# Decoding float64 weight chunks in pairs, in pieces of 512 columns, in place in a ring of four staged chunks

## The chip, the cores and the metric

The kernel runs on one core of one Trainium2 chip, in one launch. The metric is the device time of the whole program in microseconds (us). It is written by hand in a tile framework that keeps one instruction queue per engine: TensorE (PE, with its weight loads PEld), VectorE (DVE), ScalarE (ACT), GpSimd (POOL) and SyncE (SP, which issues most DMAs). Each engine runs its queue in order; an instruction that waits holds up everything behind it on its engine. The framework fixes the order in every queue when the program is built.

## The reference, cut to what matters

Three stages follow each other. The first is a recurrent attention over 4 batches, 8 heads, 768 tokens and 48 dimensions. The second is a feed-forward network on 3072 tokens, whose two weights are the subject here. The third is a mixture of 8 experts.

```
h = x @ w_in                       # w_in 384 x 2048
g = where(h > 0, h, exp(min(h, 0)) - 1)
x = g @ w_out                      # w_out 2048 x 384
```

The two weights arrive as float64 (they are drawn in float32 and multiplied by a float64 scalar). The kernel reads each float64 as two 32-bit words, the high and the low one, and forms from them the bits of a float32.

## The kernel before, in words

**Tiles.** The attention works on 24 tiles of 128 tokens (6 chunks of time, 4 batches) in four steps A1 to A4. Its result, transposed, is xT. The feed-forward network takes two tiles at a time: 12 groups of 256 tokens, each in 8 units. `ffn_in` (L537, 18 matmuls per unit into a PSUM bank psf) multiplies by one eighth of w_in, three instructions on ACT and DVE (L544, L545, L546) apply the nonlinearity, ACT and POOL split the result into a high and a low fp16 part (L548, L335), and two units later `ffn_out` (L561, 12 matmuls into the accumulators pso) multiplies by one eighth of w_out. There are three accumulators and a group uses two, so the next group needs one of them free: after the last unit of a group, L569 on ACT and L570 on DVE read them out. A mixture-of-experts stage follows with its own weights.

**The weights of the feed-forward network** stay in SBUF as fp16 pairs, wi and wo, 8 chunks of 768 columns each. These 16 chunks are made while the first group runs, in the order wi0, wi1, wi2, wo0, wi3, wo1, and so on to wo7; SEQ holds that list, and below chunk k is its k-th entry from 0. For each chunk:
- SP loads 768 KB (1536 32-bit words on each of 128 partitions) into a buffer stg (L261). There are three buffers. The load of chunk k waits until DVE has read chunk k-3 out of the buffer.
- DVE decodes it in two pieces of 384 columns with three instructions each. L283 and L284 read the high words, which lie 8 bytes apart, and leave bits in pt, a part of a PSUM accumulator bank that the first group does not use. L285 reads the low words, combines them with pt and writes float32 into a separate packed tile, sti, of which there are two buffers.
- ACT scales sti in place (L297) and copies it to the high fp16 part (L300). POOL subtracts to get the low fp16 part (L301).

**What sets the order.** A list of due times in the program (start, steps) places the attention steps among the units. The framework's own model of durations then settles the order in each engine's queue. Around the decode, DVE also runs the attention's scans (L349), masks (L449), products (L354, L355), outputs (L500, L505) and the setup of the router (L227 to L249). `early.close()` (L1070) gives back the memory of stg and sti after the first group.

## Time and profile before

| | us |
|---|---|
| median of 3 runs | 756.91 |
| lowest and highest of them | 754.46, 759.87 |
| profiled execution, its own time | 758.86 |
| its span, first to last instruction | 757.0 |

The span is divided by engine: PE is busy 94% of it, DVE 69%, ACT 65%, POOL 53%. Busy shares are averages over stages with different limits, so the stretches of the span have to be read apart. The decode of the 16 chunks lies between 12.6 and 98.8 us of the span.

### The profile page before, as it was taken

How to read it: one execution, taken by the hardware profiler on the slowest of the kernel's cores; microseconds unless marked ns; L12 is line 12 of the kernel's file. 1: busy time of each engine (PE TensorE's matmuls, PEld its weight loads, DVE VectorE, ACT ScalarE, POOL GpSimd, SP SyncE). 2: the span in 40 equal slices, each digit the busy share in tenths (PEclk: the TensorE clock that was granted, in tenths of full speed). 3: DMA queues.
4: the chain of work that ended last, by engine and by line, in shares of the span. 5: the costliest groups of instructions: out<-in, count | busy, mean ns of one | idle time of the engine just before them, and what ended most of it. 6: DMA issues, size and time to landing. Idle time of an engine off the chain costs nothing.

```text
span 757.0 us, 17652 instructions
## 1 busy us (share of the span) xinstructions
PE 710.9 (94%) x6769; PEld 536.6 (71%) x6769; DVE 521.6 (69%) x1080; ACT 490.2 (65%) x951; POOL 405.0 (53%) x414
## 2 busy tenths in 40 slices
PE   4899998999999999999999999998897999999984
PEld 4768766777777777776777777775675777777763
DVE  5999794666756675668566745776787688767751
ACT  3578646577666666666666766466744789767752
POOL 5878689778687767777767660021025433331211
PEclk9999899999999999999999999999998999999998
DMA  9975343353323432344231102199439999999820
GB/s 283 278 231 178 115 113 80 109 107 116 92 80 88 132 70 81 100 122 100 80 78 54 33 13 33 53 260 289 141 107 233 346 300 378 300 270 271 254 82 13
DMA packets 89059, 114.77 MB, mean 152 GB/s; under 512 B 60709, under 2 KB 67018, under 8 KB 88964
## 3 DMA queue, kind: packets, MB, share of 16 engines
q1 hardware_dynamic: 84512, 102.75, 48.6%
q0 software_dynamic: 3456, 10.24, 4.5%
q8 instruction: 57, 0.93, 0.5%
q10 hardware_dynamic: 996, 0.53, 0.3%
q14 instruction: 38, 0.31, 0.1%
HBM read 90.29 MB, written 9.84 MB: 132 GB/s over the span
## 4 chain that ended last, share of the span: by engine, by line
PE 55%; DMA 17%; DVE 13%; issue 6%; ACT 5%; POOL 2%; SPq 1%; POOLq 0%; DVEq 0%; ACTq 0%
PE psf L537 19%; PE pso L561 19%; DMA out_dram<-ob,idxb 7%; PE pso L894 4%; DMA SG<-in_w_dram 3%; DMA wi<-in_w_dram 3%; PE psf L874 3%; PE psa L443 2%; DVE RK L349 1%; DVE W L866 1%; ACT W L865 1%; PE psa L440 1%; DMA wi<-scr,idxa 1%; PE psa L874 1%; PE psa L519 1%
## 5 line engine op out<-in xcount | busy, mean ns | idle before, releaser
L537 PE MATMUL psf<-xT,wi 128*128 128x256 f16 x1728 | 212.6, 277 | 5.5 <-DVE e L546 3.6
L561 PE MATMUL pso<-wo,ring 128*128 128x384 f16 x1152 | 212.0, 327 | 5.9 <-DVE X L570 3.3
L537 PEld LDWEIGHTS <-wi 128*128 128x128 f16 x1728 | 167.3, 99 | 34.3 <-issue 4.5
L561 PEld LDWEIGHTS <-ring 128*128 128x128 f16 x1152 | 109.7, 98 | 69.5 <-issue 5.7
L335 POOL TENSOR_TENSOR ring<-e,ring 128x512 f16<-128x512 f32 x80 | 92.9, 1164 | 61.2 <-ACT ring L548 58.5
L546 DVE SCALAR_TENSOR_TENSOR e<-e,psf 128x512 f32<-128x512 f32 x96 | 65.7, 684 | 85.1 <-ACT e L545 79.0
L894 PE MATMUL pso<-W,gg 128*128 128x384 f16 x624 | 112.3, 328 | 1.7 <-DVE gg L335 1.6
L874 PEld LDWEIGHTS <-W 128*128 128x128 f16 x1008 | 93.4, 99 | 24.1 <-DMA XM<-G 5.0
L548 ACT ACTIVATE ring<-e 128x512 f16<-128x512 f32 x96 | 60.2, 627 | 61.1 <-DVE e L546 61.0
L894 PEld LDWEIGHTS <-gg 128*128 128x128 f16 x624 | 60.6, 98 | 37.6 <-DVE gg L335 2.9
L902 POOL DMA_INDIRECT out_dram<-ob,idxb x20 | 25.2, 1261 | 95.8 <-DVE ob L901 33.5
L544 ACT ACTIVATE e<-psf 128x512 f32<-128x512 f32 x96 | 56.5, 589 | 27.2 <-PE psf L537 23.0
L545 ACT ACTIVATE e<-e,nel 128x512 f32<-128x512 f32 x96 | 69.0, 719 | 2.5
L866 DVE SCALAR_TENSOR_TENSOR W<-wi,W 128x768 f16<-128x768 f32 x56 | 52.0, 953 | 21.7 <-ACT W L865 20.4
L866 DVE SCALAR_TENSOR_TENSOR W<-SG,W 128x768 f16<-128x768 f32 x56 | 52.5, 953 | 16.0 <-ACT W L865 15.9
L874 PE MATMUL psf<-XM,W 128*128 128x256 f16 (+1 forms) x540 | 60.5, 262 | 0.5 <-ACT mt L880 0.2
L335 DVE TENSOR_TENSOR gg<-mt,gg 128x256 f16<-128x256 f32 (+1 forms) x112 | 43.5, 402 | 22.6 <-ACT gg L881 22.0
L865 ACT ACTIVATE W<-wi 128x768 f16<-128x768 f32 x56 | 45.3, 837 | 17.7 <-DMA wi<-in_w_dram 13.4
L865 ACT ACTIVATE W<-SG 128x768 f16<-128x768 f32 x56 | 45.9, 836 | 16.3 <-DMA SG<-in_w_dram 15.1
L880 ACT ACTIVATE mt<-psf 128x256 f32<-128x256 f32 (+1 forms) x84 | 29.6, 360 | 30.8 <-PE psf L874 23.2
L881 ACT ACTIVATE gg<-mt 128x256 f16<-128x256 f32 (+1 forms) x112 | 42.6, 397 | 1.6
L349 DVE TENSOR_TENSOR_SCAN RK<-lw,bnd 112x520 f32<-112x520 f32 x24 | 34.3, 1430 | 7.0 <-ACT lw L348 4.8
(266 smaller groups left out, 1147.8 us busy)
## 6 DMA issues: line engine op xcount, KB each, us to landing
SG<-in_w_dram SPq DMA_DIRECT2D x28, 768.0 KB, 7.3
wi<-in_w_dram SPq DMA_DIRECT2D x28, 768.0 KB, 6.6
stg<-in_w_in_dram SPq DMA_DIRECT2D x8, 768.0 KB, 5.9
stg<-in_w_out_dram SPq DMA_DIRECT2D x8, 768.0 KB, 4.4
ld<-in_rk_dram SPq DMA_DIRECT2D x16, 384.0 KB, 3.2
lw<-in_w_dram SPq DMA_DIRECT2D x24, 227.5 KB, 3.2
lr<-in_r_dram SPq DMA_DIRECT2D x24, 224.0 KB, 3.6
lk<-in_k_dram SPq DMA_DIRECT2D x24, 224.0 KB, 3.1
```

The lines of the kernel that those rows point to most:

```text
L335: (nc.gpsimd if pool else nc.vector).tensor_tensor(lo, f, hi, op=ALU.subtract)
L537: mm = nc.tensor.matmul(ph[:, 256 * z_:256 * z_ + 256], lhsT=wi[:, u_, a, kk, 128 * z_:128 * z_ + 128], rhs=xg[:, b_ * KD + kk, :], start= ...
L544: nc.scalar.activation(e, ph, AF.Exp, scale=_pow2(-PH))
L545: nc.scalar.activation(e, e, AF.Identity, scale=_pow2(PH), bias=nel)
L546: LASTV[0] = nc.vector.scalar_tensor_tensor(e, e, 0.0, ph, op0=ALU.min, op1=ALU.max).ins
L548: LASTA[0] = nc.scalar.activation(hl[:, 0], e, AF.Copy).ins
L561: nc.tensor.matmul(po_[g][i][:, 0:DM], lhsT=hl[:, a, z_, 128 * i:128 * i + 128], rhs=wo[:, u_, b_, z_, :], start=(u_ + z_ + n == 0), stop= ...
L865: nc.scalar.activation(o_[:, 0], i_, AF.Copy, scale=_pow2(sc))
L866: nc.vector.scalar_tensor_tensor(o_[:, 1], i_, _pow2(sc), o_[:, 0], op0=ALU.mult, op1=ALU.subtract)
L874: nc.tensor.matmul(ph[:, 0:n_], lhsT=w_[:, a, kk, 128 * m:128 * m + 128], rhs=xm[:, b_ * KD + kk, 0:n_], start=(n == 0), stop=(n == 3 * KD ...
L881: nc.scalar.activation(h2[:, 0, m, 0:n_], t_, AF.Copy)
L894: MK[0] = nc.tensor.matmul(po[:, 0:DM], lhsT=h2[:, a, m, 128 * t:128 * t + 128], rhs=w_[:, b_, m, :], start=(m == 0 and a + b_ == 0), stop ...
```

## The change

The three buffers stg and the two buffers sti, together 24,576 bytes on each partition, become one tile stg of the same size: a ring of four chunks. Chunk k lies in slot k mod 4. Chunks 0 and 1 are decoded as before, each in two pieces of 384 columns. From chunk 2 on, an even chunk and the odd one after it lie in neighbouring slots and are decoded as one run of 1536 columns in three pieces of 512: two pieces when the even chunk's turn comes, the third when the odd one's does. The second piece covers the last 256 columns of the even chunk and the first 256 of the odd one, so both must have been loaded. pt is now a whole PSUM bank of 512 columns.

The last instruction of a piece writes the float32 over the low words, 8 bytes apart. ACT scales them there in place, ACT and POOL read them there. So a slot comes free only when POOL has subtracted its chunk. Four chunks are loaded at the start, where it was three; afterwards the loads of a pair are written in the program just before the pair's first piece.

In the changed file the three decode instructions are L275, L276 and L277, the load is L268, and the scaling, copy and subtraction are L309, L312 and L313. Every line behind them has a number higher by 12.

```diff
--- before.py
+++ after.py
@@ -254,40 +254,52 @@
     PDT = ["o2"]
     LASTD = [None]
 
+    NSG, CW = 4, 768
+    stg = s0.tile([128, NSG * CW * (2 if wide else 1)], I32 if wide else F32, name="stg", bufs=1)
+    DV = {}
+
+    def slot(k):
+        w_ = CW * (2 if wide else 1)
+        return stg[:, w_ * (k % NSG):w_ * (k % NSG) + w_]
+
     def prep_load(key):
         i = key[1]
-        src = (wiv if key[0] == 0 else wov)[i]
-        st = s0.tile([128, 768 * z], I32 if wide else F32, tag="stg", name="stg", bufs=3)
-        nc.sync.dma_start(st, src)
+        st = slot(SEQ.index(key))
+        nc.sync.dma_start(st, (wiv if key[0] == 0 else wov)[i])
         staged[key] = st
+
+    def decode(o, n):
+        sv = stg.rearrange("p (x t) -> p x t", t=2)
+        h_, l_ = sv[:, o:o + n, 1], sv[:, o:o + n, 0]
+        pt = OB[2].bitcast(I32)[:, 0:n]
+        nc.vector.tensor_scalar(pt, h_, 3, 0x3FFFFFFF, op0=ALU.logical_shift_left, op1=ALU.bitwise_and)
+        nc.vector.scalar_tensor_tensor(pt, h_, -0x40000000, pt, op0=ALU.bitwise_and, op1=ALU.bitwise_or)
+        LASTD[0] = nc.vector.scalar_tensor_tensor(
+            l_, l_, 29, pt, op0=ALU.logical_shift_right, op1=ALU.bitwise_or
+        ).ins
 
     def prep(n, dst, key, sc, mode):
         mode = int(mode)
-        if key not in staged:
-            prep_load(key)
-        st = staged[key]
         k0 = SEQ.index(key)
-        prep_(n, dst, st, sc, mode)
-        for q in range(k0 + 1, min(k0 + 1 + PLD, len(SEQ))):
+        for q in range(k0, min(k0 + (1 if k0 < 2 or k0 % 2 else 2), len(SEQ))):
             if SEQ[q] not in staged:
                 prep_load(SEQ[q])
-
-    def prep_(n, dst, st, sc, mode):
+        o = CW * (k0 % NSG)
         if wide:
-            t = s0.tile([128, 768], I32, tag="sti", name="sti")
-            sv = st.rearrange("p (x t) -> p x t", t=2)
-            hi, lo = sv[:, :, 1], sv[:, :, 0]
-            for o in (0, 384):
-                pt = psum(PDT[0]).bitcast(I32)[:, 0:384]
-                h_, l_ = hi[:, o:o + 384], lo[:, o:o + 384]
-                nc.vector.tensor_scalar(pt, h_, 3, 0x3FFFFFFF, op0=ALU.logical_shift_left, op1=ALU.bitwise_and)
-                nc.vector.scalar_tensor_tensor(pt, h_, -0x40000000, pt, op0=ALU.bitwise_and, op1=ALU.bitwise_or)
-                LASTD[0] = nc.vector.scalar_tensor_tensor(
-                    t[:, o:o + 384], l_, 29, pt, op0=ALU.logical_shift_right, op1=ALU.bitwise_or
-                ).ins
-            t = t.bitcast(F32)
+            if k0 < 2:
+                decode(o, 384)
+                decode(o + 384, 384)
+            elif k0 % 2 == 0:
+                decode(o, 512)
+                decode(o + 512, 512)
+            else:
+                decode(o + 256, 512)
+            t = stg.bitcast(F32).rearrange("p (x t) -> p x t", t=2)[:, o:o + CW, 0]
         else:
-            t = st
+            t = slot(k0)
+        prep_(n, dst, t, sc, mode)
+
+    def prep_(n, dst, t, sc, mode):
         fv = t.rearrange("p (a c) -> p a c", a=n)
         if mode == 0:
             nc.scalar.activation(dst[:, 0], fv, AF.Copy, scale=_pow2(sc))
@@ -1033,7 +1045,7 @@
             SEQ.append((0, u_))
         if u_ >= LAG:
             SEQ.append((1, u_ - LAG))
-    for key in SEQ[:3]:
+    for key in SEQ[:4]:
         prep_load(key)
     pq = [0]
 
```

DVE's queue, around the product L355 (L367 now) that ends the first use of a psf bank by the attention; RK, lw and psf are attention tiles, pso_69 is pt. Before:

```order
L283 TENSOR_SCALAR pso_69<-stg 128x384
L284 SCALAR_TENSOR_TENSOR pso_69<-stg,pso_69 128x384
L354 SCALAR_TENSOR_TENSOR RK_103<-RK_103,psf 112x8x64
L285 SCALAR_TENSOR_TENSOR sti<-stg,pso_69 128x384
L355 SCALAR_TENSOR_TENSOR RK_103<-RK_103,psf 112x8x64
```

and now:

```order
L275 TENSOR_SCALAR pso_69<-stg 128x512
L276 SCALAR_TENSOR_TENSOR pso_69<-stg,pso_69 128x512
L277 SCALAR_TENSOR_TENSOR stg<-stg,pso_69 128x512
L275 TENSOR_SCALAR pso_69<-stg 128x512
L276 SCALAR_TENSOR_TENSOR pso_69<-stg,pso_69 128x512
L277 SCALAR_TENSOR_TENSOR stg<-stg,pso_69 128x512
L366 SCALAR_TENSOR_TENSOR RK_103<-RK_103,psf 112x8x64
L275 TENSOR_SCALAR pso_69<-stg 128x512
L367 SCALAR_TENSOR_TENSOR RK_103<-RK_103,psf 112x8x64
```

In the whole queue ahead of this product stood 36 decode instructions of 384 columns (chunks 0 to 5); now 12 of 384 and 22 of 512 stand there (chunks 0 to 5, and four instructions of the pair 6 and 7).

SP's queue, around the loads of chunks 4 to 8, with what each waits for; lv, lk and lr are loads of the attention. Before:

```order
L261 DMA stg<-in_w_in_dram 128x1536 [waits DMAHW3_49,DVE_49]
L331 DMA lv<-in_v_dram 128x384 [waits DMAHW4_49,PE_49,Pool_49]
L261 DMA stg<-in_w_out_dram 128x1536 [waits DMAHW5_49,DVE_49]
L331 DMA lv<-in_v_dram 128x384 [waits DMAHW6_49,PE_49,Pool_49]
L261 DMA stg<-in_w_in_dram 128x1536 [waits DMAHW7_49,DMAHW0_49,DVE_49]
L331 DMA lk<-in_k_dram 112x512 [waits Pool_49]
L331 DMA lr<-in_r_dram 112x512 [waits DMAHW1_49,Pool_49]
```

and now:

```order
L268 DMA stg<-in_w_out_dram 128x1536 [waits DMAHW5_49,Pool_49]
L343 DMA lv<-in_v_dram 128x384 [waits DMAHW6_49,PE_49]
L268 DMA stg<-in_w_in_dram 128x1536 [waits DMAHW7_49,Pool_49]
L343 DMA lk<-in_k_dram 112x512 [waits DMAHW0_49,Pool_49]
L343 DMA lr<-in_r_dram 112x512 [waits DMAHW1_49,Pool_49]
L268 DMA stg<-in_w_out_dram 128x1536 [waits DMAHW2_49,DVE_49,Pool_49]
L268 DMA stg<-in_w_in_dram 128x1536 [waits DMAHW3_49,Pool_49]
```

The loads of the weights waited for DVE, and now wait for POOL; the attention's loads lk and lr still stand behind one of them.

ACT's queue, ahead of the first reading out of an accumulator, L569 (L581 now); X_107 is what it writes, ubc, Tk and Tr belong to the attention. Before:

```order
L471 ACTIVATE Ss_112<-US_110 112x192
L548 ACTIVATE ring<-e 128x512
L402 ACTIVATE Tk<-lk 112x512
L1074 ACTIVATE ubc<-ubc 128x384
L402 ACTIVATE Tr<-lr 112x512
L569 ACTIVATE X_107<-pso_67 128x384
```

and now:

```order
L375 ACTIVATE pso_68<-RK_103 112x4
L556 ACTIVATE e<-psf 128x512
L557 ACTIVATE e<-e,nel 128x512
L581 ACTIVATE X_107<-pso_67 128x384
L483 ACTIVATE Ss_112<-US_110 112x192
L560 ACTIVATE ring<-e 128x512
```

Tk and Tr stood ahead of the reading out, and now stand behind it; ubc is done earlier.

## Rows read from the trace of the kernel before

**Rows 1.** The page: busy us, share of the span, instructions of each engine.
```profile
PE 710.9 (94%) x6769; PEld 536.6 (71%) x6769; DVE 521.6 (69%) x1080; ACT 490.2 (65%) x951; POOL 405.0 (53%) x414
```

**Rows 2.** Busy time of each engine by stretch (x instructions), granted clock, DMA.
```profile
core 0: us, PE busy (x) PEld busy (x) DVE busy (x) ACT busy (x) POOL busy (x), PEclk, DMA share, GB/s
20.00:25.00 5.00, 5.00 (x34) 4.73 (x34) 4.93 (x6) 0.77 (x3) 5.00 (x4) 1.00 1.10 281
15.00:100.00 85.00, 78.80 (x580) 64.01 (x578) 77.39 (x138) 55.81 (x100) 64.98 (x60) 0.96 0.62 194
75.00:80.00 5.00, 4.28 (x40) 3.60 (x40) 4.93 (x10) 4.28 (x10) 4.84 (x5) 0.78 0.68 217
80.00:85.00 5.00, 5.00 (x25) 3.27 (x24) 2.87 (x6) 2.29 (x4) 2.99 (x4) 0.54 0.43 150
94.00:115.20 21.20, 18.18 (x146) 13.28 (x145) 18.84 (x29) 11.46 (x24) 16.95 (x17) 1.00 0.39 101
120.00:140.00 20.00, 19.61 (x198) 15.55 (x198) 10.28 (x18) 10.81 (x20) 15.32 (x17) 1.00 0.28 71
```

**Rows 3.** The chain of waits up to 140 us: start us, us, what.
```profile
43.11 0.69 DVE RK L355
...
43.84 3.71 PE psf L537 x18
...
80.07 3.84 PE psf L537 x18
...
113.23 0.41 ACT ubc L1074
113.65 0.52 ACT Tr L402
...
114.57 0.57 DVE X L570
...
115.19 1.14 PE pso L561 x6
```

**Rows 4.** Groups of DVE by form, to 110 us: count, busy us, mean ns, idle.
```profile
L283 DVE TENSOR_SCALAR pso<-stg 128x384 int32<-128x384 int32 x32 | 17.9, 558 | 1.7 <-DMA stg<-in_w_in_dram 1.0
L284 DVE SCALAR_TENSOR_TENSOR pso<-stg,pso 128x384 int32<-128x384 int32 x32 | 17.8, 558 | 0.7
L285 DVE SCALAR_TENSOR_TENSOR sti<-stg,pso 128x384 int32<-128x384 int32 x32 | 17.5, 548 | 1.0
...
L449 DVE SCALAR_TENSOR_TENSOR Ab<-psa,cs 128x512 f32<-128x512 f32 x8 | 5.5, 685 | 1.2 <-PE psa L440 1.2
```

**Rows 5.** Order of time (start us, us, what): first matmuls of the first group.
```profile
38.92 4.00 PE L537 MATMUL psf<-xT,wi 128*128 128x256 f16 x18 [0.90 <-ACT xT L377]
```

**Rows 6.** What DVE waited for, 12 to 116 us: us, times, longest.
```profile
DVE e L546 <- ACT e L545: 2.9, 2, 2.5
DVE X L570 <- ACT X L569: 1.9, 1, 1.9
```

**Rows 7.** Order of time, from one chunk's last decode to its subtraction.
```profile
63.73 0.55 DVE L285 SCALAR_TENSOR_TENSOR sti<-stg,pso 128x384 int32<-128x384 int32 x1
...
65.49 0.83 ACT L297 ACTIVATE sti<-sti 128x768 f32<-128x768 f32 x1
...
66.35 0.84 ACT L300 ACTIVATE wo<-sti 128x768 f16<-128x768 f32 x1
...
67.27 1.65 POOL L301 TENSOR_TENSOR wo<-sti,wo 128x768 f16<-128x768 f32 x1 [0.20 <-ACT pso L363]
```

**Rows 8.** The tile stg: time from issue to landing.
```profile
DMA to landing us min/median/max: 4.2/4.6/9.8
```

**Rows 9.** Groups of ACT at other strides and sizes, to 100 us.
```profile
L297 ACT ACTIVATE sti<-sti 128x768 f32<-128x768 f32 x16 | 13.4, 839 | 12.6 <-DVE sti L285 12.1 <-POOL Tk L400 0.4
...
L544 ACT ACTIVATE e<-psf 128x512 f32<-128x512 f32 x9 | 5.3, 589 | 6.1 <-PE psf L537 5.9 <-POOL rkp L385 0.2
...
L348 ACT ACTIVATE lw<-lw 112x104 f32<-112x104 f32 x8 | 3.1, 389 | 7.3 <-DMA lw<-in_w_dram 7.3
```

## The prediction, made before the changed kernel ran

> **What bounds the kernel now.** I read the busy times first: PE is busy 710.9 of 757.0 us [rows 1], so time is won only where PE waits, or gets its work late. Next the stretches: the change touches what runs before 115 us, and from 15 to 100 us DVE is busy 77.4 of 85 us, more than it is anywhere later for so long, while ACT has 55.8 and POOL 65.0 [rows 2]. From 94 to 115.2 us PE issues 146 matmuls in 21.2 us, from 120 to 140 us 198 in 20 [rows 2]: there PE is starved. The chain of waits says by whom [rows 3]. It runs on DVE, through the decode, up to the product L355 at 43.11 us, which frees the PSUM bank for the second unit's matmuls at 43.84. Then it runs on PE. At the end of this part it is on ACT and DVE: L570 (the second one ends at 115.1) frees an accumulator, and PE's L561 of the next group follows at 115.19. Behind that point PE's order is the same in both kernels but for small swaps and PE is nearly full (19.61 of 20 us, [rows 2]), so what this point gains or loses I carry to the end unchanged.
>
> **The change part by part.**
>
> *Fewer decode instructions.* Before: 96, with 17.9 + 17.8 + 17.5 = 53.2 us [rows 4]. Now 75: 12 of 384 columns at a mean 555 ns, and 63 of 512. For 512 columns the nearest row is L449, also reading PSUM, at 685 ns [rows 4]. 12 x 0.555 + 63 x 0.685 = 6.7 + 43.2 = 49.8 us: **-3.4 us** of DVE. The columns of all instructions add up to 36,864 in both; what goes is 21 times the fixed part of an instruction, by the two rows 685 - 512 x (685 - 558)/128 = about 177 ns, 3.7 us in all; I keep the 3.4 of the sum. [...]
>
> All of this lies on DVE's path to the second L570: what else stands ahead of it in the queue is the same, instruction for instruction, only the decode is shorter. If DVE is what holds that point, it comes 3.4 us earlier.
>
> *The order inside that path.* Ahead of L355 stood 36 decode instructions, 36 x 0.555 = 20.0 us; now 12 x 0.555 + 22 x 0.685 = 21.7. So the second unit's matmuls start 1.7 us later. The first unit's, at 38.92 [rows 5], wait for attention output that passes ACT and POOL, where the scaling, the copy and the subtraction of one more chunk now stand ahead of it: also up to 1.65 us [rows 7] late. This is not added to the sum, since it is DVE doing decode earlier rather than more. PE can take it: at the pace of 9.9 matmuls per us of 120 to 140 us, the 146 of the starved stretch need 14.7 of 21.2 us [rows 2], a slack of about 6.5 us against 1.7 + 3.4. If that cover is gone, it costs 1.7.
>
> *The reading out of the accumulator.* DVE waited 1.9 us for ACT's L569 [rows 6], behind the attention's ubc (0.41) and Tr (0.52) and Tk [rows 3]. Tk and Tr now stand behind it. The gain is between 0 and 1.9. I take **-0.5**, nearer to zero, because PE's last matmuls into that accumulator have to come earlier too.
>
> *The loads.* A slot is now freed by POOL and not by DVE. From the end of a chunk's last decode instruction (63.73 + 0.55 = 64.28) to the end of its subtraction (67.27 + 1.65 = 68.92) is 4.6 us [rows 7]; the load then takes 4.2 to 9.8, median 4.6 [rows 8]: 9.2 us, at worst 14.4. Meanwhile DVE has 12 pieces' instructions between the one that completes a chunk and the one that reads its successor in the slot: 12 x 0.685 = 8.2 us, and at the first refill also L354, L355 and L500, about 1.9 us: 10.1 us. At the median the load is hidden, by some 0.9 us; I take 0, and the worst is the first rival. Queued behind a waiting load on SP are the attention's lk and lr. Before, they stood behind a load as well.
>
> The fourth load at the start is 768 KB ahead of the attention's loads, in a stretch where the DMA engines are full and move 281 GB/s [rows 2]: 2.8 us later for those. Their first scan now stands behind one more decode instruction, and ACT's preparation of it behind the scaling of chunk 0, so I take 0; the end of the range is 2.8.
>
> *Results 8 bytes apart.* L283 and L284 already read at this stride at 558 ns for 384 columns, which is no slower than the slope of 1 ns per column says. That is the nearest row and I take 0 for all three engines. The other end is L348 on ACT, in place at 20 bytes: 389 ns for 104 columns, where the contiguous L544 and L297 give 0.98 ns per column and about 90 ns fixed [rows 9]. That is 2.9 ns per column, 2.3 us instead of 0.84 for a chunk. [...]
>
> **Sum:** -3.4 - 0.5 = -3.9 us. The profiled execution took 758.86 (span 757.0), so 755.0 for the like of it. It lies 1.95 above the median of the runs, 756.91; for the median I predict **753.0**.
>
> **The rivals.**
>
> *The refill becomes the wait* (slower). Place: the first two decode pieces of each of the six refilled pairs. DVE waits there when POOL's release and the landing together exceed about 10.1 us, that is when a load takes over 5.5 us. At 7.1 each pair costs 1.6, six of them 9.6 us: 753.0 + 9.6 = **762.6**; at the longest landing, 4.3 x 6 = 26. For it: margins under 1 us, and DVE in order, so scans and e wait too. Against it: the other work between two pairs adds cover where it is more than that of the first refill, and a stall on DVE lets ACT and POOL catch up. 15%; two in five of it beyond +1%.
>
> *The strided results are slow* (slower). Place: L309 and L312 on ACT. At L348's pace 32 instructions cost 1.5 us more each, 47 us, where ACT has 85 - 55.8 = 29 us free [rows 2]: 18 us over, 771. It decides from about 0.9 us more per instruction. Against it: L283's row. 5%.
>
> *Nothing is regained.* The late start of 1.7 us stays on PE, and PE's starved stretch is filled by something other than decode (the router's setup, POOL's backlog): **757**. For it: from 43.84 to 94 us the chain is PE's. Against it: the 6.5 us of slack. 17%.
>
> *The slow stretch of PE goes.* [...] 18%.
>
> That the change doesn't do what it says I exclude: the queue has 75 decode instructions. The forecast itself, 751 to 755, has 45%.
>
> **How the numbers follow.** About 1% (7.6 us) is what a measurement of this kernel can tell from no change. Faster by more, below 749.3: a third of the slow-stretch rival (6%), and parts of the forecast where ACT's 1.9 is won in full besides (7%): 13%. Slower by more, above 764.5: 6% of the refill rival, 3% of the strided one: 9%. The rest, 78%, within 1%. The range from 748.5 to 760.5 holds the forecast, the slow-stretch rival, the lost gain and the smaller refill waits, and leaves out under 2 in 10.
>
> **What would show it.** Right: 75 decode instructions with about 50 us, 685 ns for those of 512; L367 ending near 45.5 us; the second L582 near 111 us; no wait of DVE for stg beyond the first; L309 and L312 still near 0.84 us. Wrong: waits of DVE's L275 for the DMA of stg after 35 us (refill); ACT's L309 over 1 us (stride); L582 at 115 with an early decode (nothing regained); a granted clock of 1 from 70 to 90 us (slow stretch gone). A difference that first appears behind 140 us would mean that carrying the gain to the end was wrong.

## The result and the profile after

The change made the kernel slower. Five runs of the changed kernel beside five of the kernel before: median 771.93 us against 758.33, ratio 1.0149, 95% interval 1.0105 to 1.0192. A second series (e1): 766.72 against 758.29, ratio 1.0105 (1.0052 to 1.0159). The prediction was 753.0, with a range of 748.5 to 760.5, and gave 9% to "slower by over 1%". The profiled execution took 766.89 us (span 765.1), so it lies 5 us below the median of its series; the trace explains the loss of a run like it. Medians here and below are of all runs of a series, while ratios and intervals leave out the few runs that fell in a slower state of the chip, so that a ratio is not that of two medians.

The busy times of the page answer to [rows 1]: PE works as long as before, in a longer span.

```profile
PE 710.8 (93%) x6769; PEld 536.0 (70%) x6769; DVE 522.7 (68%) x1059; ACT 490.0 (64%) x951; POOL 408.2 (53%) x414
```

Busy time by stretch of the changed kernel, as in [rows 2] (granted clock is the column PEclk; 94 to 119.5 ends, like the stretch before, with the second reading out of an accumulator):

```profile
15.00:100.00 85.00, 71.43 (x525) 57.95 (x522) 79.15 (x109) 54.92 (x94) 65.46 (x59) 0.98 0.62 192
65.00:70.00 5.00, 2.39 (x27) 1.47 (x26) 4.01 (x7) 4.98 (x9) 3.44 (x3) 0.91 0.88 301
70.00:75.00 5.00, 4.44 (x23) 2.45 (x22) 5.00 (x11) 4.34 (x9) 3.48 (x5) 0.75 0.49 171
94.00:119.50 25.50, 23.22 (x180) 17.72 (x178) 19.25 (x30) 13.66 (x28) 23.77 (x24) 0.93 0.37 100
```

From 15 to 100 us PE is busy 7.4 us less than before (71.43, 78.80), DVE 1.8 us more (79.15, 77.39). So DVE, with 21 decode instructions fewer, is busier. The groups of DVE up to 110 us, by form, say with what; the first fence is of the kernel before:

```profile
L349 DVE TENSOR_TENSOR_SCAN RK<-lw,bnd 112x520 f32<-112x520 f32 x9 | 13.1, 1458 | 4.9 <-ACT lw L348 4.8
```

```profile
L361 DVE TENSOR_TENSOR_SCAN RK<-lw,bnd 112x520 f32<-112x520 f32 x8 | 18.8, 2345 | 4.8 <-ACT lw L360 4.8
L276 DVE SCALAR_TENSOR_TENSOR pso<-stg,pso 128x512 int32<-128x512 int32 x21 | 14.6, 693 | 0.5
L275 DVE TENSOR_SCALAR pso<-stg 128x512 int32<-128x512 int32 x21 | 14.5, 692 | 1.7 <-DMA stg<-in_w_out_dram 1.3
L277 DVE SCALAR_TENSOR_TENSOR stg<-stg,pso 128x512 int32<-128x512 int32 x21 | 14.4, 684 | 0.6
```

The decode costs what was forecast (692, 693 and 684 ns against 685). The attention's scan, which the change does not touch, takes 2345 ns in the mean instead of 1458. A mean hides how. The fourth scan of the kernel before (first fence), and that of the changed kernel with POOL's work beside it, in order of time (start us, us):

```profile
22.81 2.24 DVE L349 TENSOR_TENSOR_SCAN RK<-lw,bnd 112x520 f32<-112x520 f32 x1
```

```profile
25.13 0.68 DVE L277 SCALAR_TENSOR_TENSOR stg<-stg,pso 128x512 int32<-128x512 int32 x1
25.73 4.31 DVE L361 TENSOR_TENSOR_SCAN RK<-lw,bnd 112x520 f32<-112x520 f32 x1
...
25.18 1.30 POOL L397 TENSOR_TENSOR rkp<-lr,lk 112x512 f32<-112x512 f32 x1
26.43 1.64 POOL L313 TENSOR_TENSOR wi<-stg,wi 128x768 f16<-128x768 f32 x1
28.02 0.92 POOL L521 TENSOR_TENSOR x<-y,x 128x384 f16<-128x384 f32 x1
30.12 0.68 POOL L412 TENSOR_TENSOR Tk<-RK,lk 112x256 f32<-112x256 f32 x1 [1.18 <-DVE RK L361]
```

A scan that meets no POOL operation takes 1.24 us (the first one of the changed kernel and of the kernel before). This one ends 1.1 us after POOL's third operation in a row (28.02 + 0.92 = 28.94): by these times it all but stood still while POOL worked. The same scan before started 2.9 us earlier and took 2.24. Not every overlap costs: the changed kernel's second scan, at 7.5 us, has two POOL operations beside it and takes 1.24 us. The first of the three POOL operations had started before the scan (25.18); the other two started after it (26.43, 28.02) and ended before it all the same (28.07, 28.94; the scan at 30.04).

On the chain of waits up to 140 us these scans stand where [rows 3] had DVE's products and ACT:

```profile
25.81 4.23 DVE RK L361
...
59.85 2.28 DVE RK L361
62.15 2.60 DMA lw<-in_w_dram
...
93.84 2.32 DVE RK L361
97.12 3.06 DVE RK L361
```

The other rows: first matmul of the first group ([rows 5]), DVE's waits ([rows 6]), landing of stg ([rows 8]), ACT's operations on the results 8 bytes apart ([rows 9]), and, from 12 to 116 us, what the loads on SP's queue waited for (L268 are those of the weights).

```profile
42.65 0.59 PE L549 MATMUL psf<-xT,wi 128*128 128x256 f16 x2 [1.04 <-ACT xT L389]
```

```profile
DVE X L236 <- DMA X<-in_mod_dram: 3.4, 1, 3.4
...
DVE e L558 <- ACT e L557: 2.6, 1, 2.6
DVE pso L275 <- DMA stg<-in_w_out_dram: 1.3, 2, 0.8
```

```profile
DMA to landing us min/median/max: 4.2/4.9/10.7
```

```profile
L309 ACT ACTIVATE stg<-stg 128x768 f32<-128x768 f32 x16 | 14.7, 916 | 11.6 <-DVE stg L277 11.6
L312 ACT ACTIVATE wi<-stg 128x768 f16<-128x768 f32 x8 | 7.2, 906 | 0.0
```

```profile
SPq L343 <- DVE RK L361: 17.1, 6, 5.5
SPq L268 <- POOL wi L313: 15.2, 5, 7.5
...
SPq L268 <- POOL wo L313: 9.7, 5, 2.8
```

The first matmul comes 3.7 us late (42.65, 38.92 before). Below, **the shift** of a kernel is how much later one and the same matmul starts than in the first profile of the kernel before. For the changed kernel it is +3.7 at the first, +10.2 at the 73rd L537 (66.06 before), +4.7 at 135 us (the 145th L561), +5.0 at 379, +1.5 at 548 and +8.1 at the last matmul. So the loss of this profile has two parts: one made in the first 115 us, and one that comes and goes in the expert stage.

### The profile page after: what moved, and what is told of

Read it like the earlier page. It is cut to its first block, busy times and chain, and to the rows that moved or that the text cites. A ratio compares the mean times of both kernels' runs of the same rounds, so it can differ in the third digit from the quotient of the medians.

```text
span 765.1 us, 17641 instructions
## 1 busy us (share of the span) xinstructions
PE 710.8 (93%) x6769; PEld 536.0 (70%) x6769; DVE 522.7 (68%) x1059; ACT 490.0 (64%) x951; POOL 408.2 (53%) x414
## 4 chain that ended last, share of the span: by engine, by line
PE 49%; DMA 21%; DVE 14%; issue 7%; ACT 4%; POOL 4%; SPq 1%; POOLq 0%; DVEq 0%; ACTq 0%
PE psf L549 17%; PE pso L573 17%; DMA out_dram<-ob,idxb 7%; DMA SG<-in_w_dram 6%; PE pso L906 3%; DVE W L878 3%; DVE RK L361 3%; DMA wi<-in_w_dram 2%; PE psf L886 2%; PE psa L455 1%; POOL ring L347 1%; DMA lw<-in_w_dram 1%; DVE e L558 1%; PE psa L886 1%; DMA ld<-in_rk_dram 1%
## 5 line engine op out<-in xcount | busy, mean ns | idle before, releaser
L347 POOL TENSOR_TENSOR ring<-e,ring 128x512 f16<-128x512 f32 x80 | 92.6, 1160 | 62.5 <-ACT ring L560 59.5
L886 PEld LDWEIGHTS <-W 128*128 128x128 f16 x1008 | 93.6, 99 | 26.6 <-issue 5.4
L556 ACT ACTIVATE e<-psf 128x512 f32<-128x512 f32 x96 | 56.6, 589 | 26.8 <-PE psf L549 22.5
L878 DVE SCALAR_TENSOR_TENSOR W<-wi,W 128x768 f16<-128x768 f32 x56 | 52.0, 954 | 20.8 <-ACT W L877 19.1
L877 ACT ACTIVATE W<-wi 128x768 f16<-128x768 f32 x56 | 45.0, 836 | 15.2 <-DMA wi<-in_w_dram 12.2
L347 DVE TENSOR_TENSOR gg<-mt,gg 128x256 f16<-128x256 f32 (+1 forms) x112 | 43.4, 402 | 13.7 <-ACT gg L893 12.2
L361 DVE TENSOR_TENSOR_SCAN RK<-lw,bnd 112x520 f32<-112x520 f32 x24 | 42.0, 1750 | 7.0 <-ACT lw L360 4.8
L892 ACT ACTIVATE mt<-psf 128x256 f32<-128x256 f32 (+1 forms) x84 | 29.3, 359 | 23.3 <-PE psf L886 11.5
```

Of the source, the lines that this page charges most:

```text
L347: (nc.gpsimd if pool else nc.vector).tensor_tensor(lo, f, hi, op=ALU.subtract)
L361: nc.vector.tensor_tensor_scan(flat(PR), lw, bnd, 0.0, op0=ALU.mult, op1=ALU.add)
L556: nc.scalar.activation(e, ph, AF.Exp, scale=_pow2(-PH))
L877: nc.scalar.activation(o_[:, 0], i_, AF.Copy, scale=_pow2(sc))
L878: nc.vector.scalar_tensor_tensor(o_[:, 1], i_, _pow2(sc), o_[:, 0], op0=ALU.mult, op1=ALU.subtract)
L886: nc.tensor.matmul(ph[:, 0:n_], lhsT=w_[:, a, kk, 128 * m:128 * m + 128], rhs=xm[:, b_ * KD + kk, 0:n_], start=(n == 0), stop=(n == 3 * KD ...
```

## The experiments

The expectations name theories by letters: R, the refills that wait for POOL; S, the collision of scan and POOL; O, the order of the decode; W, the results 8 bytes apart; Q, the attention's loads held up on SP behind a refill; P, the chunks themselves coming late; M, chance in the expert stage; F in e1, that stage following the shift, and in e17 and e18 the fourth load; I, the ring itself.

Each line of the table is one profile of one kernel. "Freed by" is the engine whose reading is the last that SP's refill of a slot waits for. A line has the loads at the start, the shifts at the first matmul, at 135, at 379 us and at the last (us), and the ratio of the runs with its 95% interval.

| kernel | loads | freed by | first | 135 | 379 | last | ratio |
|---|---|---|---|---|---|---|---|
| changed kernel | 4 | POOL | 3.7 | 4.7 | 5.0 | 8.1 | 1.0149 (1.0105–1.0192) |
| e1 the same again | 4 | POOL | 3.4 | 2.5 | 2.3 | 5.2 | 1.0105 (1.0052–1.0159) |
| e2 ring, no pairs | 4 | POOL | 4.3 | 10.0 | 9.9 | 9.3 | 1.0120 (1.0067–1.0173) |
| e3 packed in a pair | 4 | DVE, POOL | 3.0 | 2.9 | 3.8 | 4.6 | 1.0027 (0.9993–1.0060) |
| e4 pairs from 6 | 4 | POOL | 4.0 | 4.4 | 6.4 | 6.0 | 1.0052 (1.0021–1.0082) |
| e5 packed in a slot | 4 | POOL | 4.0 | 3.6 | 6.5 | 7.9 | 1.0121 (1.0080–1.0162) |
| e6 e5 without pairs | 4 | POOL | 3.1 | 7.5 | 9.6 | 14.5 | 1.0181 (1.0124–1.0238) |
| e9 refills on POOL's queue | 4 | POOL | 4.7 | 8.1 | 9.2 | 9.6 | 1.0191 (1.0138–1.0243) |
| e10 before, same edit | 3 | DVE, sent by POOL | 2.9 | 9.2 | 9.8 | 8.8 | 1.0134 (1.0078–1.0191) |
| e16 freed by ACT | 4 | ACT, DVE | 3.5 | 4.5 | 7.9 | 5.2 | 1.0062 (1.0020–1.0104) |
| e17 three loads | 3 | POOL | 1.1 | 1.5 | 4.4 | 3.6 | 1.0071 (1.0037–1.0105) |
| e18 before, fourth load | 4 | DVE | -2.1 | -1.0 | 6.3 | 8.5 | 1.0054 (1.0016–1.0092) |
| e11 pairs, no ring | 3 | DVE | -0.1 | -1.5 | -1.6 | 0.2 | 0.9964 (0.9925–1.0003) |
| e12 before again | 3 | DVE | -0.6 | -0.6 | -0.6 | 2.2 | 0.9971 (0.9931–1.0011) |
| e13 before, copy of stg | 3 | DVE | -0.7 | -1.7 | 1.2 | 2.4 | 1.0072 (1.0036–1.0108) |
| e14 before, copy of sti | 3 | DVE | -0.7 | -0.3 | 3.6 | 8.4 | 1.0021 (0.9986–1.0056) |
| e15 e11, copy of stg | 3 | DVE | -0.4 | -5.7 | -6.1 | -8.4 | 0.9964 (0.9930–0.9998) |

### Is it the pairs, the strides or the release? (e1 to e4)

e1 has no edit. 

> The changed kernel a second time, to see which part of its loss comes back. All theories: first matmul of L549 (L537 before) again 3 to 4 us later than before, and 4 to 5 us later at 135 us and up to 500 us, since the first 115 us hold no run-to-run chance. Theory M (the other 3 us that grew behind 600 us in the expert stage are chance of its weight DMAs): the end of this profile is anywhere from 3 to 9 us late, with the growth at other places. Theory F (they follow from the shift): the same growth at the same waits, end 7.5 to 9 us late. Time 764 to 773 us.

766.72 us. The first matmul came back within 0.4 us, the shift at 135 us within 2.3; the last part did not (5.2 against 8.1). The chance of the early stage is larger than "none", as I had put it.

e2:

```diff
-        for q in range(k0, min(k0 + (1 if k0 < 2 or k0 % 2 else 2), len(SEQ))):
+        for q in range(k0, k0 + 1):
...
-            elif k0 % 2 == 0:
-                decode(o, 512)
-                decode(o + 512, 512)
-            else:
-                decode(o + 256, 512)
```

with the branch of two pieces of 384 taken for every chunk. 

> Ring of four, results over the low words, refills behind POOL: all kept; pairing and the 512-column pieces taken out (each chunk 2 pieces of 384, its load when its turn comes). Theory S+O (pairing brings decode pieces forward and bunches POOL's subtractions under the scans of L361): the scans up to 110 us take 13 to 15 us together as before (18.8 in the changed kernel), first matmul of L549 within 1 us of before, time 757 to 762 us; what is left is ACT's 0.07 us per operation on strided results, 2.3 us. Theory R (refills released by POOL hold up DVE and the queue): the loss stays, DVE waits for stg again, 767 to 773 us.

768.69 us. Without pairs the loss stays and the shift at 135 us is 10.0: the loss does not need the pairs. The scans up to 110 us took 13.7 us in all, as S+O had it, and yet nothing was won, so the sum of the scans does not rank kernels.

e3: the last instruction of a piece writes words side by side from the pair's first word.

```diff
+        b_ = 1536 * (o // 1536)
+        r_ = stg[:, o + b_:o + b_ + n]
...
-            l_, l_, 29, pt, op0=ALU.logical_shift_right, op1=ALU.bitwise_or
+            r_, l_, 29, pt, op0=ALU.logical_shift_right, op1=ALU.bitwise_or
```

> Pairs and 512-column pieces kept; the results are written side by side over the first half of a pair's own words instead of over every second word. So ACT and POOL read packed words, and the slot of the pair's second chunk is free when DVE has decoded the pair, not when POOL has subtracted. Theory R with W (strided results): half of the refills no longer wait for POOL, ACT's L309 and L312 back at 0.84 us from 0.91: the shift at 135 us falls from 4.7 to 1 to 3 us, time 760 to 766 us. Theory S+O (order and scans): the scans up to 110 us still take 17 us or more, the shift at 135 us stays 3.5 to 5 us, 766 to 772 us.

761.69 us, ACT back at 837 ns; the shift at 135 us, 2.9, is not below e1's 2.5. In the runs most of the loss is gone. The time and the shift lie where R with W put them; the scans up to 110 us, which S+O left at 17 us or more, took 14.0.

e4:

```diff
-            if k0 < 2:
+            if k0 < 6:
```

and the same in the line of the loads. 

> The changed kernel, but chunks 0 to 5 are decoded one by one in 384-column pieces, and pairs begin with chunk 6 (decode 81 instructions instead of 75, about 1.1 us more DVE). Theory O (pieces brought forward ahead of L366/L367 of the second chunk of attention cost 1.7 us, and set up the 4.3 us scan): first matmul of L549 within 1.5 us of before instead of 3.7 later, the scan at 25.7 us back at 1.6 to 2.3 us, the shift at 135 us 1 to 3 us instead of 4.7, time 760 to 766 us. Theory R (the refills): only the first two refill waits change, shift at 135 us 4 to 5 us, 767 to 773 us.

763.36 us, but neither the first matmul (4.0 late) nor the early scan (3.85 us) moved. O's mechanism fails; its time, 760 to 766 us, is met for a reason that the run does not show.

### Strides against release (e5, e6)

e5 packs each chunk's results into the first half of its own slot, the middle piece in two blocks of 256:

```diff
+        b_, c_ = 1536 * (o // CW), o % CW
+        r_ = stg[:, b_ + c_:b_ + c_ + n]
...
+        if c_ + n > CW:
+            r_ = stg[:, b_ + c_:b_ + c_ + 2048].rearrange("p (a c) -> p a c", a=2)[:, :, 0:256]
...
```

> Pairs and 512-column pieces kept, results packed over the first half of each chunk's own slot (the middle piece in two blocks), so that ACT and POOL read packed words but every slot still waits for POOL's subtraction. Theory W (the strided results cost ACT and POOL): as far down as e3_packed_in_place, 760 to 763 us, ACT's L309 and L312 at 0.84 us. Theory R (it was the slots that POOL frees late): stays near the changed kernel, 766 to 770 us, with DVE waiting for stg as in it. If both bear half: 763 to 766 us.

767.33 us with ACT at 838 and 839 ns. The 0.07 us of the stride are 2.3 us of ACT in 32 instructions, and not the loss. e5 and e3 differ in what frees the second slot of a pair (POOL or DVE): 1.0121 against 1.0027, the intervals apart. That is no clean proof of R: at 135 us their profiles are only 0.7 us apart (3.6, 2.9), 3.8 us of e5 are lost between 190 and 200 us, behind the decode, and e5's scans up to 110 us took 20.4 us against 14.0.

e6 is e5 with e2's edit. 

> As e2_ring_no_pairs (2 pieces of 384, each load at its turn), but results packed over the first half of the chunk's own slot: against the kernel before, only the ring is left (four slots freed by POOL instead of three freed by DVE). Theory W: 757 to 761 us, the 9.9 us shift at 135 us of e2 falls below 3. Theory R: 765 to 770 us, the shift at 135 us stays over 6 us.

772.31 us, shift 7.5: the shift is as R expects, the time lies above its 765 to 770 us.

### The collision by itself (e7, e8)

The edit in both, here for the subtraction:

```diff
-        nc.gpsimd.tensor_tensor(dst[:, 1], fv, dst[:, 0], op=ALU.subtract)
+        nc.gpsimd.tensor_scalar(dst[:, 1], fv, 0.0, None, op0=ALU.mult)
```

> The changed kernel with every GpSimd tensor operation of the decode and of the attention (L313, L347, L397, L412, L470, L471, L476, L480) reading one tensor instead of two: the low words become zeros and products lose a factor, so the values are not the reference's, and only times up to the end of the attention are compared, with the same edit in the kernel before beside it. Theory S (a scan with two sources on VectorE and a two-source GpSimd operation shut each other out): the scans of L361 are all 1.2 to 1.4 us, those up to 110 us 11 to 12 us together instead of 18.8, and the first matmul of L549 comes 1 to 2 us after that of the kernel before with the same edit (3.0 to 3.7 now). Without S: scans of 2 to 4 us stay.

> The kernel before with the same edit as in e7_after_one_source (the same parts of the values left out). Theory S: its scans go from 1.43 us mean to 1.24, 1.5 us less up to 110 us, so that e7 minus e8 at 135 us is 0 to 2 us where the changed kernel stood 2.4 and 4.7 us behind. If the collisions cost nothing in the end (theory R or W alone), e7 stays 2.5 to 5 us behind e8 at 135 us.

791.65 and 780.70 us; at 135 us e7 stood 25 us behind e8. The test failed as a test of the loss: in e8 POOL's operation with one source takes 2213 to 2262 ns in the mean (most single ones 2.13 us) where the subtraction took 1645 to 1660, and all that waits for POOL is later. As a measurement of the collision it can be read. Scans of e8 (first fence: all 24 of them, min/median/max ns; second: two of them, and what POOL did):

```profile
L352 DVE TENSOR_TENSOR_SCAN RK<-lw,bnd x24: 1226/1242/2432, 4.7 to 435.8; 112x520 f32<-112x520 f32 x24
```

```profile
17.93 1.23 DVE L352 TENSOR_TENSOR_SCAN RK<-lw,bnd 112x520 f32<-112x520 f32 x1
...
20.13 1.23 DVE L352 TENSOR_TENSOR_SCAN RK<-lw,bnd 112x520 f32<-112x520 f32 x1
...
18.31 2.78 POOL L301 TENSOR_SCALAR wi<-sti 128x768 f16<-128x768 f32 x1
```

Both scans lie beside POOL operations that read one SBUF tile. They keep their 1.23 us, and POOL pays: this L301 took 2.78 us, most others of the kind 2.13. Of the 24 scans of e7 none took over 1.73 us; the three of e8 above that (1.86, 2.10, 2.43) overlap the two-source subtractions that were left in. So the scans over 1.73 us lie beside two-source operations; beside one-source operations alone the longest took 1.73 us (e7), and beside two-source ones some of e8 took no more than 1.25. The second scan here started 1.8 us after L301 (20.13, 18.31) and was not held up for it.

### The queue, and pairs without the ring (e9 to e12)

e9:

```diff
-        nc.sync.dma_start(st, (wiv if key[0] == 0 else wov)[i])
+        q = nc.sync if SEQ.index(key) < NSG else nc.gpsimd
+        q.dma_start(st, (wiv if key[0] == 0 else wov)[i])
```

> The changed kernel, only that the staged loads from the fifth on are issued on GpSimd's own queue, behind its own subtractions, instead of on SP. A slot is still freed by the subtraction, but SP's other loads (attention's w, r, k, v) no longer stand behind that wait. Theory Q (SP held by a refill that waits for POOL brings attention's loads late): 758 to 763 us, ACT's waits for lw and lv at most 2.5 us each, shift at 135 us under 2. Theory P (the chunks themselves come late to DVE, since their slots come free late): 766 to 772 us, DVE still waits for stg.

e10 is the kernel before with the same edit. 

> Control: the kernel before with the same edit (loads from the fourth on issued on GpSimd's queue). The slots are freed by DVE. If the queue by itself gains or costs something it shows here: 756 to 761 us if it is neutral. Theory Q then reads e9 against this run: within 3 us of it. A POOL that waits for DVE before it can issue may cost 2 to 5 us.

774.61 and 770.44 us: both theories of e9 are off, because the control itself lost 1.3%. In e10 DVE frees the slots as before, but the refill goes out when POOL comes to it: the loads of chunks 9 to 11 at 59.0, 61.2 and 68.2 us, where the kernel before has 48.9, 53.9 and 59.3. So a kernel without a ring can be 9.2 us late at 135 us. That the late refills did it is not shown: POOL also spends time on each of its 13 loads (556 to 759 ns, below), and the attention's loads on SP go out at other times (one of lw at 65.7 us instead of 56.0).

```profile
L262 POOL DMA_DIRECT2D stg<-in_w_out_dram x8: 556/579/759, 18.6 to 91.7; - x8
```

e11: three staged slots, results packed in three slots sti, pairs where two slots are neighbours.

```diff
-    NSG, CW = 4, 768
+    NSG, CW = 3, 768
...
-            l_, l_, 29, pt, op0=ALU.logical_shift_right, op1=ALU.bitwise_or
+            sti[:, o:o + n], l_, 29, pt, op0=ALU.logical_shift_right, op1=ALU.bitwise_or
```

> Pairing and 512-column pieces without the ring's release: three staged slots freed by DVE as before, results packed in three slots of their own, four pairs (chunks 3 and 4, 6 and 7, 9 and 10, 12 and 13; 84 decode instructions instead of 96 or 75). Theory R (the release by POOL is the loss): 754 to 759 us, at or below the kernel before, shift at 135 us within 1.5 us. Theory O (pairing itself costs, by the order on DVE and the scans): 762 to 768 us, shift at 135 us 2.5 to 5.

757.24 us, shift -1.5: as R expects. These four pairs save 12 instructions, by the prediction's 177 ns 2.1 us; the gain is within the noise, as the next run says, so that it does not contradict this sum and does not show it. And e11 holds the longest scan of all, with POOL beside it:

```profile
56.92 5.67 DVE L361 TENSOR_TENSOR_SCAN RK<-lw,bnd 112x520 f32<-112x520 f32 x1
...
55.50 1.66 POOL L313 TENSOR_TENSOR wi<-sti,wi 128x768 f16<-128x768 f32 x1
57.10 1.66 POOL L313 TENSOR_TENSOR wo<-sti,wo 128x768 f16<-128x768 f32 x1
58.71 1.17 POOL L347 TENSOR_TENSOR ring<-e,ring 128x512 f16<-128x512 f32 x1
59.82 1.66 POOL L313 TENSOR_TENSOR wi<-sti,wi 128x768 f16<-128x768 f32 x1
```

It passed with no loss at 135 us: a long scan does not by itself decide the time.

e12 has no edit. 

> The kernel before once more, for a second profile of it: how much of the growth behind 600 us (3 us in the changed kernel's first profile, 2.8, -0.6, 1.8 and -0.5 in four others) two profiles of one kernel differ by. Theory M (chance of the expert stage's weight loads): the two profiles of before differ by up to 3 us behind 520 us and by less than 0.5 us up to 135 us. Time 754 to 762 us, ratio 1 within its interval.

759.35 us, ratio 0.9971. Two profiles of one kernel: -0.6 at 135 us, +2.2 at the end. So M holds for 2 to 3 us of the expert stage, and a ratio of 0.9964 is not "faster".

### The release alone (e13 to e16)

e13, in the kernel before:

```diff
         nc.gpsimd.tensor_tensor(dst[:, 1], fv, dst[:, 0], op=ALU.subtract)
+        nc.gpsimd.tensor_copy(tn, st[:, 0:1])
```

e14 reads one column of `fv` instead; e15 is e13's line in e11. 

> The kernel before, plus one copy of a single column on GpSimd behind each subtraction, which reads the chunk's staged tile: so a staged slot comes free when GpSimd has passed, and nothing else of the change is there (no pairs, no ring, results packed in tiles of their own, three slots). Theory R (the release by GpSimd is the loss): 766 to 778 us, ratio 1.01 to 1.025, chunks 6 to 9 ready 4 us or more later than before, shift at 135 us over 3. If the release is harmless and the ring's layout or the in-place writing is the loss: 757 to 761 us, like the control e14.

> Control for e13: the same copy of one column on GpSimd, but of the decoded tile, which GpSimd reads anyway; the staged slot is still freed by DVE. All theories: 756 to 761 us, shift at 135 us within 1.5 us. If it costs 4 us or more, the copies themselves or a new order disturb the stage, and e13 is read against it.

> e11_pairs_slots_freed_by_dve plus the one-column copy of the staged slot on GpSimd: pairs, packed results of their own, slots freed by GpSimd. Theory R: back to a loss, 764 to 776 us, shift at 135 us over 3 where e11 had -1.5. Otherwise 755 to 760 us.

764.62, 761.47 and 756.51 us. e13 and e15 did not do what they were made for. The scheduler put the copy where its input is ready, ahead of the chunk's subtraction, and SP's refills still wait for DVE last (33.0 us in 11 waits in e13; e15 below):

```profile
L315 POOL COPY tn<-stg x16: 173/185/1147, 16.0 to 83.3; 128x1 int32<-128x1 int32 x16
```

```profile
SPq L269 <- DVE sti L278: 29.7, 10, 4.8
```

So they are two more kernels with DVE's release, in another order of instructions, and say nothing on R. They show what an order is worth: a copy of one column moved the last matmul by -8.6 us against e11, the expert stage's chance included, and, in e13, the runs by 0.7%.

e16:

```diff
-        nc.gpsimd.tensor_tensor(dst[:, 1], fv, dst[:, 0], op=ALU.subtract)
+        nc.gpsimd.tensor_tensor(dst[:, 1], dst[:, 0], dst[:, 0], op=ALU.subtract)
```

> The changed kernel with GpSimd's subtraction reading the high half twice instead of the decoded chunk and the high half (the low words become zeros, so the values are not the reference's; same engine, same number of sources): a slot of the ring is freed by ACT's copy L312, before GpSimd comes to it. Theory R: shift at 135 us falls to 0 to 2 us (2.4 to 4.7 in the changed kernel), 758 to 764 us. If the ring or the strided writing is the loss: shift and time stay, 766 to 771 us. The expert stage may route other rows, so the shift at 135 us is read first.

767.30 us, ratio 1.0062, shift 4.5. SP's waits for a slot now end with ACT six times and with DVE five times:

```profile
SPq L268 <- DVE stg L277: 7.9, 5, 2.8
```

The shift did not fall to 0 to 2 us, so R fails in the profile. The ratio is below both of the changed kernel's, though its interval overlaps e1's, so in the runs part of R may hold. It stays open between R and the ring; the four loads at the start were still there.

### The fourth load (e17, e18)

e17:

```diff
-    for key in SEQ[:4]:
+    for key in SEQ[:3]:
         prep_load(key)
```

> The changed kernel with three staged loads at the start instead of four; the fourth goes out at its turn, behind the loads of the third attention tile. Theory F (the fourth load stands ahead of the third tile's w on SP, the scheduler puts ACT's scaling of that w, L360, behind the chunk's L312, and the scan starts 2.9 us late and under three GpSimd operations): ACT's order at the start is that of the kernel before, the fourth scan starts at 22 to 23 us and takes 2.2 us (25.7 and 4.3 in the changed kernel), first matmul of L549 within 1 us of before, shift at 135 us below 1.5, time 755 to 762 us. Theory I (the ring itself, its in-place results or release): the shift at 135 us stays 2.4 to 5 us, 765 to 771 us.

ACT's queue at the start, behind the first chunk's scaling, in the changed kernel and in e17; lw is prepared for a scan by L360:

```
changed kernel                              e17
L312 ACTIVATE wi<-stg 128x768               L360 ACTIVATE lw<-lw 112x104
L360 ACTIVATE lw<-lw 112x104                L312 ACTIVATE wi<-stg 128x768
L375 ACTIVATE pso_68<-RK_103 112x4          L375 ACTIVATE pso_68<-RK_103 112x4
L309 ACTIVATE stg<-stg 128x768              L360 ACTIVATE lw<-lw 112x104
L431 ACTIVATE gg<-psf,cs 128x448            L309 ACTIVATE stg<-stg 128x768
L360 ACTIVATE lw<-lw 112x104                L431 ACTIVATE gg<-psf,cs 128x448
```

e17's order is that of the kernel before. Its third and fourth scan and the first matmul, in order of time:

```profile
18.84 1.64 DVE L361 TENSOR_TENSOR_SCAN RK<-lw,bnd 112x520 f32<-112x520 f32 x1 [0.18 <-ACT lw L360]
...
22.02 2.25 DVE L361 TENSOR_TENSOR_SCAN RK<-lw,bnd 112x520 f32<-112x520 f32 x1
```

```profile
39.99 0.80 PE L549 MATMUL psf<-xT,wi 128*128 128x256 f16 x3 [1.38 <-ACT xT L389]
```

The scan is back at 22.02 us and 2.25 us long, the first matmul at +1.1 instead of +3.4 and +3.7. That much of F is shown. The time, 765.55 us, misses F's 755 to 762 and lies in I's 765 to 771, and 0.7% stay; by its interval e17 is not clear of e1.

e18, in the kernel before:

```diff
     for key in SEQ[:3]:
         prep_load(key)
+    nc.sync.dma_start(xt_, wov[7][:, 0:1408])
```

> The kernel before with one more load behind the three staged loads at the start, of 92% of a chunk's bytes (1408 of 1536 words a row) into a tile that nobody reads: the fourth load alone, without pairs or ring. Theory F: ACT's order as in the changed kernel, fourth scan near 25.5 us and 3.8 to 4.4 us long, first matmul of L538 (L537 before) 3 to 4.5 us late, time 764 to 772 us. Theory I: first matmul within 1 us, 757 to 761 us.

ACT's order changed as in the changed kernel, but the fourth scan started at 24.27 and took 1.45 us, and the first matmul came 2.1 us early. 763.21 us, below F's 764 to 772, and its loss came behind 138 us: 3.7 us by 156 us, and 3.7 more between 190 and 200. So the fourth load changes the order; what that order costs differs from kernel to kernel: the scan took 4.31 us in the changed kernel and 1.45 here.

## Why the prediction was wrong

**The step that failed** is "what else stands ahead of it in the queue is the same, instruction for instruction, only the decode is shorter". The same instructions did not take the same time, and were not ready at the same time. DVE's time up to the start of the ninth scan, summed from its rows (each from the end of the one before; in brackets the number of instructions):

| us | idle | decode | 8 scans | other | ninth scan starts |
|---|---|---|---|---|---|
| before | 15.2 | 50.3 | 11.5 | 32.8 (59) | 109.6 |
| changed kernel | 19.8 | 48.0 | 18.3 | 26.6 (54) | 112.5 |
| e1 | 16.6 | 47.9 | 19.1 | 26.8 (54) | 110.3 |
| e17 | 15.2 | 47.7 | 15.3 | 29.6 (55) | 107.8 |
| e15 | 12.3 | 48.9 | 12.8 | 29.2 (55) | 103.1 |

Decode gave 2.3 us, the scans took 6.8, waiting 4.6; five other instructions moved behind the point. The second L582 ended at 119.4 us instead of the forecast 111 (115.1 before), in e1 at 117.2: the size differs from profile to profile, the lost gain does not. That DVE spent its gain on scans and waits is measured; that these alone hold the point is not, since e2 and e3 have shorter scans (13.2 and 13.5 us) and are late too.

**The fourth load at the start: "I take 0".** Wrong. e17 against the two profiles of the changed kernel gives 2.3 to 2.7 us at the first matmul and 0.9 to 3.2 at 135 us. The range's upper end, 2.8, is close by luck: it was the time of 768 KB on the DMA queue, and what came was a new order on ACT and a scan that started 2.9 us later and met three POOL operations. The prediction had seen the scan behind one more decode instruction and ACT's preparation behind chunk 0 (it stands behind the copy L312), and did not price what the new start would meet.

**The loads: "At the median the load is hidden".** For DVE's direct wait nearly right: 1.3 us in the changed kernel, 0.4 in e1. Yet at 135 us all seven kernels whose slots are freed by DVE and refilled by SP (before and e12 among them; e7 and e8 are left out) lie between -5.7 and 0, and all others, where POOL or ACT frees or sends, between +1.5 and +10.0. In the changed kernel the loads of chunks 10 and 11 go out at 57.9 and 64.4 us, 4.0 and 5.1 later than before (that of chunk 9 1.1 earlier). e10 is the only one of the others without a ring, and all but e10 and e17 have the fourth load too. So the grouping supports that a refill behind POOL brings this part late. It is not shown by a clean test: e13 and e15, made for it, did not make POOL free the slots, and e16 speaks against it.

**The order inside the path** (1.7 us late, L367 ending near 45.5 us): in e17 it ended at 45.1 and the first matmul came 1.1 late, which agrees; in the changed kernel, with the fourth load, it ended at 47.7. **Reading out** (-0.5): the wait of 1.9 us for L569 [rows 6] is gone, but DVE waited 3.4 us for the DMA of X instead (0.3 before). **Stride** (0): 916 and 906 ns against 839, 0.07 us each and not the loss (e5); the 771 of that rival is the right number by a wrong mechanism. **Slow stretch** (18%): no run shows a gain by a clock that PE keeps because other waits stand before it. The granted clock of the changed kernel is 1.00 from 75 to 85 us (0.78 and 0.54 before, [rows 2]), but 0.91 and 0.75 from 65 to 75 us (1.00 before) and 0.93 from 94 to 119.5 us: the stretch did not go but moved.

**Carried to the end unchanged.** It held from 135 to 500 us in the changed kernel (4.7 to 5.0) and failed in the expert stage, where the shift went to 1.5 and 8.1. It also failed at 190 us in eight other kernels: e4, e5, e6, e13, e14, e16, e17 and e18 lose 2 to 4 us there, the two profiles of the changed kernel nothing. It looks like the same collision. e17 first, then e1, around the same scan:

```profile
188.32 3.68 DVE L361 TENSOR_TENSOR_SCAN RK<-lw,bnd 112x520 f32<-112x520 f32 x1 [0.23 <-ACT pso L375]
...
188.32 0.51 POOL L480 TENSOR_TENSOR US<-US,dmc 112x192 f32<-112x192 f32 x1
188.79 1.00 POOL L470 TENSOR_TENSOR ld<-ld 128x384 f32<-128x384 f32 x1
189.74 1.16 POOL L347 TENSOR_TENSOR ring<-e,ring 128x512 f16<-128x512 f32 x1
190.86 2.09 POOL L347 TENSOR_TENSOR Tk<-lk,Tk 112x512 f16<-112x512 f32 x1
```

```profile
189.24 1.61 DVE L361 TENSOR_TENSOR_SCAN RK<-lw,bnd 112x520 f32<-112x520 f32 x1 [0.23 <-ACT pso L375]
...
189.24 0.51 POOL L480 TENSOR_TENSOR US<-US,dmc 112x192 f32<-112x192 f32 x1
189.75 1.89 POOL L470 TENSOR_TENSOR ld<-ld 128x384 f32<-128x384 f32 x1
```

Scan and POOL's L480 start together in both. By these times the scan of e1 gets in behind L480, and L470 is stretched (1.89 us, 1.00 in e17); in e17 L470 follows at once, then L347; the scan gets in behind them, takes 3.68 us, and the second L347 is stretched (2.09 us, 1.15 in e1). PE then waited 2.4 us for DVE's L582 instead of 0.3, and its clock fell:

```profile
199.00:204.00 5.00, 5.00 (x31) 3.77 (x30) 2.08 (x4) 3.87 (x8) 1.16 (x1) 0.69 0.67 157
```

The like stretch of e1 has 1.00. From 190 to 200 us the shift of e17 grows by 3.7 us, that of e1 by nothing. DVE and POOL start the same operations in the same order around this scan in nine profiles that show 1.60 or 1.61 us and in eight that show 3.67 or 3.68 (e15 shows 1.24; e7 and e8 are left out). Whether chance or the kernel decides is not shown: the two kernels that were profiled twice gave 1.6 us both times.

**What stays open.** The 0.7% that e17 still loses; how much of the changed kernel's 11 us (median 769.2 of its 11 runs against 758.3) is the early shift (2.5 and 4.7 in its profiles) and how much the scan at 190 us or the expert stage in runs that have no profile; whether POOL's release costs by itself; and whether the ring costs anything beside its refills. No kernel tried was shown to beat the kernel before: e15's interval ends at 0.9998, and e12, with no edit, has 0.9971.

## What to carry to other kernels

Fewer instructions on a busy engine are worth what its other instructions let through: before summing counts times durations, look at the single durations of one untouched instruction (here 1.24 to 4.31 us for the same scan), and find what stands beside the long ones. Change one thing at a time: four pairs alone (e11) cost nothing that the runs show; bundled with a ring, a later release and a fourth load, pairs came with a loss of 1 to 1.5%. And where a scheduler fixes the order, a load added at the head of a queue is an edit of every engine's order.

## What the runs showed that was not expected

A scan with two SBUF sources can all but stand still while POOL runs two-source operations back to back: 1.24 us alone, 3.68 and 4.31 behind three of them, 5.67 behind four, and 1.23 beside a one-source operation, which was stretched instead (2.78 us, most others 2.13). At the same place in the same local order it took 1.61 us in some kernels and 3.68 in others. One-source tensor_scalar on POOL is slower than the two-source subtraction it replaced (2213 to 2262 ns in the mean in e8 against 1645 to 1660 in the kernel before, 128x768).
